# Second half of batch 0 by full-height matmuls, its values regrouped by transfers, expert 1's first chunk earlier

## The chip, the cores and the metric

The kernel runs on one core of a Trainium2 chip. The metric is the device time of one execution in microseconds (us); lower is better. A core has a matrix engine (PE, TensorE), three engines for element work (DVE, ACT, POOL), and SP, which issues transfers. POOL issues transfers too, and these can change the number type on the way. Each engine takes its instructions in a fixed order; between engines, semaphores tell when a result is there or a buffer is free. PE writes into PSUM, and ACT or DVE copy from there into SBUF, the working memory.

## The reference

The input is `q`, `k`, `v` of shape (4 batches, 8 heads, 768 tokens, 64), a small matrix `sort_net` of 8x8 for each batch and head, and a mixture of four experts.

```python
P = sort_net                                  # (B, H, 8, 8)
for _ in range(5):                            # rows and columns normalized in turn
    P = exp(P - max(P, -1)); P = P / (sum(P, -1) + 1e-9); P = P / (sum(P, -2) + 1e-9)
k_sorted[b,h,i] = sum_j P[b,h,i,j] * k_block[b,h,j]      # blocks of 96 tokens
v_sorted[b,h,i] = sum_j P[b,h,i,j] * v_block[b,h,j]
attn = softmax(q_block k_sorted^T / 8)        # 96x96 inside each of the 8 blocks
x = attn v_sorted                             # (3072 tokens, 512): heads side by side
p = domain_probs / sum(domain_probs)          # (3072, 4)
out = sum_e p[:, e] * (relu(x @ w1[e]) @ w2[e])          # 512 -> 1024 -> 512
```

## The kernel before

All matrix work is in 16 bits with float sums. Batch 0 has code of its own, since the experts can't begin before its attention is there; batches 1 to 3 run their attention in slots between the matmuls of the experts (`PLANS`).

**Mixing as a matmul.** A head's keys lie in SBUF as 128 rows (8 blocks j times 16) of 6x64 values: token p*6+r is row p, part r. The mixing of blocks is then a product with a matrix that holds P[i,j] where the row inside the block agrees. `PI0[hf]` is this matrix for half `hf` of the output blocks (four of eight), 64 columns for a head, built from `maskk` and `Rs`.

**Batch 0 by halves.** Half 0 is the first four output blocks (tokens 0 to 383), half 1 the other four. The heads are in two quads (`qd`), each of two pairs (`sg`) of two heads (`hh`). For a quad and a half there are these steps (names as in the code):

- `h_q`: 24 transposes of 64x64 bring the queries into `qT0`.
- `h_k` and `h_v`: 24 matmuls each (`mix_half`, L495) with outputs of 64 partitions by 64 columns, then one copy (`mixed`, L506) into `kT` or `vT0`. The values come out with channels on partitions.
- `h_w`: 8 transposes (L522) turn the values to tokens on partitions, and a copy (L527) puts them into `vs0s`, beside a column of ones that gives the softmax sums.
- `h_s(qd, qq)`: scores of two blocks, 8 matmuls (L550) and one exponential on ACT (L556). `qq` is 0, 1 in half 0 and 2, 3 in half 1.
- `h_a(qd, qq)`: the product with the values, 8 matmuls (L567), then on DVE a reciprocal (L580) and a multiplication (L581) into `xsl`.
- `h_x(qq)`: 4 matmuls for each quad (L598) bring the result into `xT`, the input of the experts; the copy (L602) is on ACT or DVE.

PSUM results of these steps rotate through `psa`, a pool of two buffers; expert work has `psm`, another two. `ps_a10` is a buffer of `psa` that is used under several names (`ps_s11` too), the last time by `h_x(1, vec, [1], ps_s11)`.

**Experts for batch 0.** Expert 0 is done plainly: `group0` (L679) is its first layer for one half, `second_layer0` (L714) its second, one token tile of 128 after the other, each result scaled by `p_sb` on DVE (L723). Experts 1 to 3 go by chunks of 256 tokens: `chunk_first` (L790) is their first layer, two groups of 16 matmuls, each followed by a DVE step (L796) that applies relu and the weight row `pbs`. The second layers of these experts use sums of blocks (`h_sums`, `weight_sums`) and `product`.

**The order around the change.** After `h_a(1, 1)` come the two `h_k(qd, 1)`, with the groups of expert 0 between; then `h_v(0, 1)`, `h_q(0, 1)` and `second_layer0(0, next_stages)`. This calls `next_stages` after 4 and after 8 matmuls of each of its three tiles, and `chunk_first(0, 0, [1, 2], ...)` calls it after each of its four groups. Each call takes one entry of the list `later` (L1439): the rest of half 1's queries and values, its scores, its products, and at last `h_x(2)` and `h_x(3)`. `h_x(3)` stands before the last group of expert 2. Then `first_layer0(2, 2)` (L679) reads `xT` of half 1.

**Transfers.** POOL's queue has the loads of the weights (`load_w1`, `load_w2`) in the order of need, with tables between them (`builds`, the `memset` of `vo`, `maskv`). SP's queue has the way of the weights p: `spread_weights` is advanced by `next(p_steps)`; its last step multiplies, stores p to `p_dram`, loads `p_0` (expert 0's, as 6 rows of 128), the broadcast rows of all four experts (`load_p`) and stores the rest. `own_weights` turns `p_0` by a transpose on PE (L249). `load_p_one` follows for the second chunk.

**Borrowed room.** `Tt` are four tiles for the sums of expert weights, which are made later; until then they hold `q0` (in `Tt[3]`) and `p_in`, `p_out`, `p_0` (in `Tt[2]`).

## Time and profile before

| what | value |
|---|---|
| runs | 359.24, 359.61, 359.78 us; median 359.61 |
| span of the profiled execution | 357.8 us, 1.8 under the median of the runs |
| PE busy | 351.6 us (98%), clock 1.00 |
| DVE, ACT, POOL busy | 276.2, 170.6, 133.6 us |
| DMA share in the first 140 us | 8 to 9 tenths or more of 16 engines for nearly all of it |

The span runs from the first to the last instruction; what lies around it is not in the profile, and no time for the profiled execution itself is given beside the span. In the lines of the profile a row of the timeline has the start in us, the duration in us, engine, line, operation, output<-input, size, and the count of instructions that were merged into it. In brackets stands how long the engine was idle before it and what it waited for. Matmuls overlap, so the time that a group costs is the distance from its start to the next start. A row of windows has the stretch, then its length, then for each engine the busy time and the number of instructions, the TensorE clock that was granted, the DMA share and GB/s. A row of transfers has the queue that issued them, their count, the KB of each and the median us from issue to landing.

### The profile page before, as it was taken

The numbers are of one execution on the slowest core, as the hardware profiler recorded it, in microseconds if no ns is written. First come the engines' busy times: TensorE is split into PE (matmuls) and PEld (weight loads), VectorE is DVE, ScalarE is ACT, GpSimd is POOL, SyncE is SP. The second block draws the span as 40 slices with busy tenths as digits, with TensorE's granted clock in tenths as the row PEclk, the third lists the DMA queues.
The fourth block names the chain that finished last, engine by engine and source line by source line (L and its number), as shares of the span: only waits on it lengthen the run. The fifth ranks groups of instructions, "written<-read, shape, count | busy, mean of one in ns | idle before, by whom it ended". The sixth has DMA issues, their size and how long they took to land.

```text
span 357.8 us, 9498 instructions
## 1 busy us (share of the span) xinstructions
PE 351.6 (98%) x3949; PEld 306.3 (86%) x3949; DVE 276.2 (77%) x552; ACT 170.6 (48%) x303; POOL 133.6 (37%) x149
## 2 busy tenths in 40 slices
PE   8899999999999999999999999999999999999996
PEld 8686867888888888888899988888888888888886
DVE  5754797869889587868978988896678886588963
ACT  2554240442434535367947258830288611688201
POOL 8864010375122222000535318840058800188400
PEclk9999999999999999999999999999999999999999
DMA  8999999999999999935996420005200015100011
GB/s 114 207 205 228 216 210 198 209 163 165 201 154 160 188 152 170 194 74 73 168 201 90 102 78 0 2 2 108 102 29 2 3 39 138 61 0 2 2 73 46
DMA packets 72022, 40.51 MB, mean 113 GB/s; under 512 B 40614, under 2 KB 66732, under 8 KB 71980
## 3 DMA queue, kind: packets, MB, share of 16 engines
q0 software_dynamic: 36576, 19.93, 41.9%
q1 hardware_dynamic: 35260, 19.92, 28.5%
q8 instruction: 31, 0.51, 0.6%
q14 instruction: 11, 0.09, 0.1%
q10 hardware_dynamic: 144, 0.07, 0.1%
HBM read 42.13 MB, written 6.34 MB: 135 GB/s over the span
## 4 chain that ended last, share of the span: by engine, by line
PE 95%; DVE 2%; ACT 1%; DMA 0%; issue 0%; DVEq 0%
PE ps_h L790 18%; PE ps_Q L1264 18%; PE ps_p L774 12%; PE ps_X L1121 10%; PE ps_Z L1121 7%; PE ps_Q L1121 7%; PE ps_Z L1264 6%; PE ps_h L679 3%; PE ps_o L714 3%; PE ps_p L830 3%; PE ps_a L453 2%; PE ps_s L418 2%; PE ps_k L399 1%; PE ps_v L365 1%; PE ps_a L567 1%; PE ps_mk L495 1%
## 5 line engine op out<-in xcount | busy, mean ns | idle before, releaser
L790 PE MATMUL ps_h<-xT,w 128*128 128x256 f16 x576 | 67.5, 273 | 0.0
L790 PEld LDWEIGHTS <-w 128*128 128x128 f16 x576 | 55.2, 98 | 7.2
L796 DVE SCALAR_TENSOR_TENSOR Hb<-ps_h,pb 128x1024 f16<-128x1024 f32 x34 | 41.5, 1223 | 17.2 <-PE ps_h L790 15.8
L1121 PEld LDWEIGHTS <-w 128*128 128x128 f16 x480 | 43.6, 98 | 4.8
L1134 POOL TENSOR_TENSOR arena<-tmp,pb 128x512 f16<-128x512 f32 x12 | 15.2, 1275 | 65.7 <-PE ps_Z L1121 49.8
L1264 PEld LDWEIGHTS <-Hb 128*128 128x128 f16 x320 | 31.1, 98 | 3.5
L1133 ACT ACTIVATE tmp<-tmp 128x512 f32<-128x512 f32 x46 | 29.0, 632 | 3.9 <-DVE tmp L1171 3.9
L1264 PEld LDWEIGHTS <-Sb 128*128 128x128 f16 x304 | 28.3, 98 | 3.0
L1121 PEld LDWEIGHTS <-arena 128*128 128x128 f16 x312 | 27.7, 98 | 2.9
L425 ACT ACTIVATE ET<-ps_s 96x768 f16<-96x768 f32 x24 | 18.0, 802 | 25.1 <-PE ps_s L418 24.8
L121 POOL DMA_DIRECT2D arena<-in_q_dram x24 | 19.9, 838 | 25.5 <-DMA q_ring<-arena 25.2
L408 ACT CAST kT<-ps_k 64x384 f16<-64x384 f32 x48 | 22.7, 473 | 13.3 <-PE ps_k L399 12.3
L1121 PE MATMUL ps_X<-ET,arena 128*128 128x256 f16 x168 | 25.2, 272 | 0.0
L1264 PE MATMUL ps_Q<-w,Hb 128*128 128x256 f16 x192 | 24.6, 273 | 0.0
L774 PEld LDWEIGHTS <-Hb 128*128 128x128 f16 x232 | 21.8, 98 | 3.0
L1127 DVE SCALAR_TENSOR_TENSOR Hb<-ps_X,pb 128x512 f16<-128x512 f32 x27 | 18.7, 691 | 7.0 <-PE ps_X L1121 7.0
L1141 ACT COPY ps_X<-ps_Z 128x512 f32<-128x512 f32 x27 | 15.4, 571 | 17.8 <-PE ps_Z L1121 17.8
L1121 PE MATMUL ps_Z<-xT,w 128*128 128x256 f16 (+1 forms) x176 | 22.5, 258 | 0.0
L760 DVE TENSOR_TENSOR Sb<-Hb 128x512 f16<-128x512 f16 x33 | 20.6, 647 | 0.0
L1148 ACT COPY tmp<-ps_X 128x512 f32<-128x512 f32 x26 | 15.2, 585 | 9.2 <-PE ps_X L1121 6.6
L1127 DVE SCALAR_TENSOR_TENSOR Hb<-ps_Z,pb 128x512 f16<-128x512 f32 x27 | 18.4, 682 | 1.3 <-PE ps_Z L1121 1.3
L1171 DVE TENSOR_TENSOR tmp<-ps_Q,tmp 128x512 f32<-128x512 f32 x26 | 17.8, 683 | 0.8 <-PE ps_Q L1121 0.8
(266 smaller groups left out, 741.6 us busy)
## 6 DMA issues: line engine op xcount, KB each, us to landing
w<-in_moe_w_dram POOLq DMA_DIRECT2D x6, 1024.0 KB, 27.9
pb<-p_dram SPq DMA_DIRECT2D x9, 512.0 KB, 7.0
arena<-in_k_dram POOLq DMA_DIRECT2D x8, 384.0 KB, 9.3
arena<-in_v_dram POOLq DMA_DIRECT2D x8, 384.0 KB, 7.5
vs<-arena SPq DMA_DIRECT2D x36, 66.0 KB, 4.9
arena<-in_q_dram POOLq DMA_DIRECT2D x24, 96.0 KB, 7.5
out_dram<-ob SPq DMA_DIRECT2D x9, 256.0 KB, 2.0
w<-in_moe_w_dram POOLq DMA_DIRECT2D x4, 512.0 KB, 12.5
```

The lines of the kernel that those rows point to most:

```text
L121: nc.gpsimd.dma_start(t[:, h // 2, :, h % 2, :], q[b, h].rearrange("(t p) d -> p t d", p=P))
L408: nc.scalar.copy(kT[ds(D * hh, D), r], pk[ds(D * r, D), hh].rearrange("p a (i c) -> p a i c", c=CP),)
L425: nc.scalar.activation(ETs[2 * (pr % 2) + hh][:, 0:S].rearrange("c (a x) -> c a x", a=2), pss[hh][0:BLK, :, 0:HS], AF.Exp, bias=0.0, scale ...
L760: tt(sm[0], blk(0, 1), blk(1, 1), ALU.add)
L774: nc.tensor.matmul(ps, lhs(e, f), Ts[e][rhs][:, f, :], start=(first and e == es[0] and f == 0), stop=(done and e == es[-1] and f == KH - 1 ...
L790: nc.tensor.matmul(ps[:, f, :], w1sb[e][:, kc, ds((4 * g + f) * P, P)], xT[:, kc, ds(2 * c * P, 2 * P)], start=(kc == 0), stop=(kc == NKC ...
L796: nc.vector.scalar_tensor_tensor(out=Hb[:, homes.get(e, e), ds(4 * g, 4), :], in0=ps[:], scalar=0.0, op0=ALU.max, in1=weights(e).broadcast ...
L1121: nc.tensor.matmul(dst[:, ds(f * cols, cols)], a[lhs][:, k, ds((f0 + f) * P, P)], t[rhs][:, k, :], start=(first and f == 0 and k == 0), st ...
L1127: nc.vector.scalar_tensor_tensor(out=home(i, j), in0=src.rearrange("p (f x) -> p f x", f=m), scalar=0.0, op0=ALU.max, in1=weight(j).broadc ...
L1133: nc.scalar.activation(src, src, AF.Relu, bias=0.0, scale=1.0)
L1171: tt(t12, Q, u2, ALU.add)
L1264: nc.tensor.matmul(ps, lhs(e, f), Ts[e][rhs][:, f, part], start=(first and e == 0 and f == 0), stop=(e == E - 1 and f == KH - 1), skip_gro ...
```

## The change

The queries, keys and values of half 1 are done in another way, and the steps around them are put in another order.

- `half_v` replaces `h_v` and `h_w` for half 1: two matmuls for a pair of heads, each with 64 columns of weights (`PIv1`, 4 output blocks times 16) and 384 columns of values. Tokens come out on partitions at once, but as 16 times 4 (c, i). A copy on ACT puts them into `vo1s[qd]`; after the quad's second pair six transfers on SP (one for each r) regroup them into `vs1s[qd]`, 96 partitions. `vs1s` and one of `vo1s` lie in `Tt[0]` and `Tt[1]`. `PIv1` lies in `Tt[2]` and is built on POOL, from `maskv`.
- `half_k` replaces `h_k` for half 1: 12 matmuls with 128 by 128 weights (two parts r at a time) and 64 columns, and four copies.
- `pair_q` and `half_q` replace `h_q` for half 1: two copies on ACT into `q1`, 12 full transposes for both quads, and two copies on DVE.
- `h_a` for half 1 reads `vs1s`.
- POOL's `maskv`, the build of `PIv1` and the two `memset` of `vo1s` stand ahead of `load_w1(1)`; before, `maskv` and one `memset` stood behind `load_w1(2)`.
- The weight rows of chunk 0 come one expert at a time; `spread_weights` has two steps more, taken between the parts of `half_v`, so that SP has the row of expert 1, six value transfers, the row of expert 2, six more, the row of expert 3 and the rest of the store. The row of expert 0 is not loaded for batch 0.
- `own_weights` is a plain float matmul of 128 rows (`p_0` has zeros below its 6 rows) in place of a transpose.
- `second_layer0` takes the tiles to do: two tiles, then expert 1's first chunk, the third tile, then expert 2's. The list `later` is new, and its last entries are `h_a(1, 2)` with `h_a(1, 3)`, and `h_x(2)` with `h_x(3)`.

```diff
@@ -206,18 +206,27 @@
 
     p_dram = dramp.tile([E, N], F32, name="p_dram")
     p_sb = const.tile([P, R, 1], F32, name="p_sb")
-    p_0 = p_part(2 * E * NT + NT, P)[0:R]
-    ident6 = p_part(2 * E * NT + NT + P, R)[0:R]
+    p_0 = p_part(2 * E * NT + NT, P)
+    ident6 = p_part(2 * E * NT + NT + P, R)
+    nc.gpsimd.memset(p_0, 0.0)
     S_P = S // NT
 
     pbs = {}
 
+    def load_p_rows(pb, b, c, es):
+        nc.sync.dma_start(
+            pb[:, es],
+            p_dram[es, ds(b * S + 2 * c * P, 2 * P)].rearrange("(o e) x -> o e x", o=1).broadcast_to(
+                [P, es.stop - es.start, 2 * P]
+            ),
+        )
+
+    def new_p(b, c):
+        return moe.tile([P, E, 2 * P], F32, name=f"pb_{b}_{c}", tag="pb", bufs=1)
+
     def load_p(b, c):
-        pb = moe.tile([P, E, 2 * P], F32, name=f"pb_{b}_{c}", tag="pb", bufs=1)
-        nc.sync.dma_start(
-            pb[:],
-            p_dram[:, ds(b * S + 2 * c * P, 2 * P)].rearrange("(o e) x -> o e x", o=1).broadcast_to([P, E, 2 * P]),
-        )
+        pb = new_p(b, c)
+        load_p_rows(pb, b, c, slice(0 if b else 1, E))
         return pb
 
     def load_p_one(b, c, e):
@@ -239,14 +248,18 @@
         )
         p_rows = p_dram.rearrange("e (p t) -> p e t", t=NT)
         nc.sync.dma_start(p_rows[0:S_P], p_out[0:S_P])
-        nc.sync.dma_start(p_0, p_dram[0, 0:S].rearrange("(t p) -> t p", p=P))
-        pbs[(0, 0)] = load_p(0, 0)
+        nc.sync.dma_start(p_0[0:R], p_dram[0, 0:S].rearrange("(t p) -> t p", p=P))
+        pbs[(0, 0)] = new_p(0, 0)
+        for e in range(1, E):
+            load_p_rows(pbs[(0, 0)], 0, 0, slice(e, e + 1))
+            if e < E - 1:
+                yield
         nc.sync.dma_start(p_rows[S_P:P], p_out[S_P:P])
         yield
 
     def own_weights(ps):
 
-        nc.tensor.transpose(ps, p_0, ident6)
+        nc.tensor.matmul(ps, p_0, ident6, start=True, stop=True)
         nc.vector.tensor_copy(p_sb.rearrange("p t o -> p (t o)"), ps)
 
 
@@ -279,7 +292,7 @@
     sn16 = const.tile([GH, NB, NB, CP], F16, name="sn16")
     warm(84)
     p_steps = spread_weights()
-    nc.gpsimd.tensor_copy(ident6, ident[0:R, 0:R])
+    nc.gpsimd.tensor_copy(ident6, ident[:, 0:R])
     for it in range(5):
         nc.scalar.activation(sn[:], sn[:], AF.Exp, bias=0.0, scale=1.0)
         if it == 4:
@@ -514,6 +527,88 @@
     def h_v(qd, hf, copy, pool=psa):
         mixed("v", qd, mix_half("v", qd, hf, pool), 0, HB, copy)
 
+    def flat_T(e, at, n):
+        return Tt[e].rearrange("p a f x -> p (a f x)")[:, ds(at, n)]
+
+    NVO, NVS, NQ1 = R * 4 * VW, HB * 4 * VW, 2 * R * P
+    vo1s = [vo, flat_T(0, 0, NVO).rearrange("p (r h w) -> p r h w", r=R, h=4)]
+    vs1s = [
+        flat_T(e, at, NVS)[0:BLK].rearrange("c (i s h w) -> c i s h w", i=HB, s=2, h=2)
+        for e, at in ((0, NVO), (1, NQ1))
+    ]
+    PIv1 = flat_T(2, 3 * KH * DH - H * CP * HB, H * CP * HB).rearrange("p (h c i) -> p h c i", h=H, i=HB)
+
+    def build_PIv1(eng):
+        eng.tensor_tensor(
+            PIv1,
+            maskv.rearrange("p (o c i) -> p o c i", o=1, i=NB)[:, :, :, 0:HB].broadcast_to([P, H, CP, HB]),
+            Rs[:, 0:H, HB:NB].rearrange("p g (o i) -> p g o i", o=1).broadcast_to([P, H, CP, HB]),
+            ALU.mult,
+        )
+
+    def half_v(qd, sg, copy):
+
+        ps = psa([P, 2, 512], F32, f"ps_v0_{qd}_{sg}")[0:CP * HB]
+        for hh in range(2):
+            h = 2 * sg + hh
+            nc.tensor.matmul(
+                ps[:, hh, 0:R * D],
+                PIv1[:, 4 * qd + h].rearrange("p c i -> p (c i)"),
+                head(0, "v", 4 * qd + h).rearrange("p r d -> p (r d)"),
+                start=True, stop=True,
+            )
+        vo1 = vo1s[qd][0:CP * HB]
+        copy(
+            vo1[:, :, ds(2 * sg, 2), 0:D],
+            ps[:, :, 0:R * D].rearrange("p h (r d) -> p r h d", r=R),
+        )
+        if sg:
+            for r in range(R):
+                nc.sync.dma_start(
+                    vs1s[qd][ds(r * CP, CP)].rearrange("c i s h w -> c (i s h w)"),
+                    vo1[:, r].rearrange("p h w -> p (h w)"),
+                )
+
+    def half_k(qd, copy):
+
+        ps = psa([P, 2, 512], F32, f"ps_k0_{qd}")
+        pk = ps[:, :, 0:R * 64].rearrange("p h (x i c) -> p h x i c", x=R, c=CP)
+        for hh in range(2):
+            for sg in range(2):
+                h = 4 * qd + 2 * sg + hh
+                for a in range(R // 2):
+                    nc.tensor.matmul(
+                        ps[:, hh, ds((sg * (R // 2) + a) * 64, 64)],
+                        head(0, "k", h)[:, ds(2 * a, 2), :].rearrange("p r d -> p (r d)"),
+                        PI0[1][:, h, :, :].rearrange("p i c -> p (i c)"),
+                        start=True, stop=True,
+                    )
+        kT = kTs[qd][:, 0:S].rearrange("p (i x r c) -> p r x i c", i=HB, r=2, c=CP)
+        for hh in range(2):
+            for r in range(2):
+                copy(kT[ds(D * hh, D), r], pk[ds(D * r, D), hh])
+
+    q1 = flat_T(1, 0, NQ1).rearrange("p (s r x) -> p s r x", s=2, r=R)
+
+    def pair_q(sg):
+
+        nc.scalar.copy(
+            q1[:, sg].rearrange("p r (h d) -> p r h d", h=2),
+            q0[:, 1, ds(2 * sg, 2)].rearrange("p h r d -> p r h d"),
+        )
+
+    def half_q(copy):
+
+        ps = psa([P, 2, 1024], F16, "ps_q1")
+        for sg in range(2):
+            for r in range(R):
+                nc.tensor.transpose(ps[:, sg, ds(r * P, P)], q1[:, sg, r], ident[:])
+        for qd in range(2):
+            copy(
+                qT0[qd][:, :, 1],
+                ps[:, :, 0:R * P].rearrange("p s (r q x) -> p s r q x", r=R, q=2)[:, :, :, qd],
+            )
+
     def h_w(qd, copy, i0=0, n=HB, at=None):
 
         ps = psa([P, n, 2 * P], F16, f"ps_w_{state['n']}") if at is None else at
@@ -567,7 +662,7 @@
                 nc.tensor.matmul(
                     ps[:, hh, ds(n * VW, D + 1)],
                     ET[:, ds((4 * hh + n) * BLK, P)],
-                    vs0s[qd][:, 2 * (qq % 2) + n % 2, n // 2, hh, 0:D + 1],
+                    (vs0s, vs1s)[qq // 2][qd][:, 2 * (qq % 2) + n % 2, n // 2, hh, 0:D + 1],
                     start=True, stop=True,
                 )
 
@@ -705,8 +800,8 @@
             group0(qq, nq, g)
             slot()
 
-    def second_layer0(hf, slot):
-        for t in range(R // 2):
+    def second_layer0(hf, slot, ts=range(R // 2)):
+        for t in ts:
             col = (R // 2) * hf + t
             po = psm([P, 2, 512], F32, f"ps_o_{col}")
             ps = po[:, 0, 0:Dm]
@@ -1373,6 +1468,13 @@
     load_half_queries(1)
     load_w2(0, 2)
     build_PI0(nc.gpsimd, 1, 0, H, Rs[:, 0:H, HB:NB])
+    nc.gpsimd.tensor_copy(
+        maskv.rearrange("p (c i) -> p c i", i=NB),
+        eye16.rearrange("p (c o) -> p c o", o=1).broadcast_to([P, CP, NB]),
+    )
+    build_PIv1(nc.gpsimd)
+    for t in vo1s:
+        nc.gpsimd.memset(t[:, :, :, ds(D, 2)], 1.0)
     h_w(0, vec, 0, 2, tails[("v", 0, 0)])
     mixed("v", 0, mv0, 2, 2, vec)
     mk1 = mix_half("k", 1, 0, psm)
@@ -1407,23 +1509,22 @@
     h_x(1, act, [0], ps_s01)
     evacuate00()
     group0(0, 1, 1, [2, 3])
+    load_w1(1)
+    load_w1(2)
     h_a(1, 1, ps_s11)
-    h_k(0, 1, act)
+    half_v(0, 0, act)
     group0(1, 1, 0, [0, 1])
+    half_v(0, 1, act)
+    next(p_steps)
     h_x(1, vec, [1], ps_s11)
     group0(1, 1, 1, [0, 1])
-    h_k(1, 1, vec)
+    half_v(1, 0, act)
     group0(1, 1, 0, [2, 3])
+    half_v(1, 1, act)
+    next(p_steps)
     group0(1, 1, 1, [2, 3])
-
-
-    load_w1(1)
-    load_w1(2)
-    nc.gpsimd.memset(vo[:, :, :, ds(D, 2)], 1.0)
-    nc.gpsimd.tensor_copy(
-        maskv.rearrange("p (c i) -> p c i", i=NB),
-        eye16.rearrange("p (c o) -> p c o", o=1).broadcast_to([P, CP, NB]),
-    )
+    for sg in range(2):
+        pair_q(sg)
 
     def builds(b):
         for n in range(2 * b, 2 * b + 2):
@@ -1437,15 +1538,16 @@
     builds(1)
 
     later = [
-        [(h_q, 1, 1, vec)],
-        [(h_v, 1, 1, act)],
-        [(h_s, 0, 2), (h_w, 1, vec)],
-        [(h_w, 0, vec), (h_s, 1, 2)],
+        [(half_k, 1, act)],
+        [(half_q, vec)],
+        [(h_s, 0, 2)],
+        [(h_s, 1, 2)],
+        [(h_s, 0, 3)],
+        [(h_s, 1, 3)],
         [(h_a, 0, 2)],
-        [(h_s, 0, 3), (h_a, 1, 2)],
-        [(h_s, 1, 3), (h_a, 0, 3)],
-        [(h_x, 2, act), (h_a, 1, 3)],
-        [(h_x, 3, act)],
+        [(h_a, 0, 3)],
+        [(h_a, 1, 2), (h_a, 1, 3)],
+        [(h_x, 2, act), (h_x, 3, act)],
     ]
 
     def next_stages():
@@ -1453,14 +1555,15 @@
             for f, *args in later.pop(0):
                 f(*args)
 
-    h_v(0, 1, act)
-    h_q(0, 1, vec)
-    second_layer0(0, next_stages)
+    half_k(0, vec)
+    second_layer0(0, next_stages, range(2))
+    chunk_first(0, 0, [1], 1, next_stages)
+    second_layer0(0, next_stages, range(2, 3))
     load_queries(1, range(2))
     for qd in range(2):
         for nm in ("v", "k"):
             load_natural(1, nm, qd)
-    chunk_first(0, 0, [1, 2], 1, next_stages)
+    chunk_first(0, 0, [2], 1, next_stages)
     pb_1 = load_p_one(0, 1, 1)
     h_sums(1, 4)
     for w in range(1, 5):
```

## The prediction

> **What bounds the kernel now.** I read the page's busy times and its chain first, then the stage that the change touches by windows, then that stage's timeline on each engine, then the DMA view.
>
> ```profile
> PE 351.6 (98%) x3949; PEld 306.3 (86%) x3949; DVE 276.2 (77%) x552; ACT 170.6 (48%) x303; POOL 133.6 (37%) x149
> ...
> PE 95%; DVE 2%; ACT 1%; DMA 0%; issue 0%; DVEq 0%
> ```
> TensorE is busy for the whole span and is 95% of the chain that ends last. A microsecond taken from its queue is worth a microsecond, but so is a gap put into it.
>
> ```profile
> 23.20:46.20 23.00, 23.00 (x376) 17.48 (x374) 14.45 (x24) 9.93 (x13) 8.51 (x10) 1.00 1.20 219
> ```
> The stage that changes runs from the end of head group 1's second attention product (23.52 us) to the layer of expert 0's second half (46.19). In this window TensorE (first busy figure) is busy for 23.00 of 23.00 us, at clock 1.00; DVE has 14.45, ACT 9.93. No TensorE wait over 0.2 us stands in it, nor any after 46.2. The stage has no slack to win, only work.
>
> ```profile
> 23.52 0.57 PE L495 MATMUL ps_mk<-Sb,arena 128*64 128x64 f16 x24
> 24.02 0.83 PE L679 MATMUL ps_h<-xT,w 128*128 128x192 f16 x8
> ...
> 29.50 0.56 PE L271 MATMUL ps_q<-ident,T 64*64 64x64 f16 x24
> 30.00 1.04 PE L714 MATMUL ps_o<-w,Hb 128*128 128x512 f16 x4
> ...
> 32.87 0.65 PE L522 MATMUL ps_w<-ident,Sb 128*96 128x128 f16 x8
> 33.35 1.03 PE L714 MATMUL ps_o<-w,Hb 128*128 128x512 f16 x4
> ...
> 44.10 0.51 PE L598 MATMUL ps_x<-perm,xsl 96*128 96x96 f16 x8
> 44.44 1.91 PE L790 MATMUL ps_h<-xT,w 128*128 128x256 f16 x16
> 46.19 5.54 PE L679 MATMUL ps_h<-xT,w 128*128 128x384 f16 x32
> ...
> 65.05 0.49 PE L365 MATMUL ps_v<-arena 128*128 128x384 f16 x2
> 65.37 1.47 PE L830 MATMUL ps_p<-w,Hb 128*128 128x256 f16 x12
> ```
> Start to start gives what a group costs: 24 half-width products 0.50 us, 24 query transposes 0.50, 8 value transposes 0.48. The last h_x ends before 16 expert matmuls (44.44), which cover the copy of its result; only then does the next layer read it.
>
> **TensorE's work.** Removed for the second half: h_k twice, h_v twice, h_q twice at 0.50 each, h_w at 0.48 and 0.54: 4.02 us. Added:
> - half_v, 4 calls of two 384-column matmuls: row 65.05, 0.33 each (0.32 to 0.33 start to start): 1.32.
> - half_k, 2 calls of 12 matmuls of 64 columns. No row has 128 rows by 64 columns; bounds are 21 ns (L495, 0.50/24) and 55 ns (128 columns, L399, 6 in 0.33). The h_a products with 65 columns are nearest, 8 in 0.25, 31 ns: 0.74 in all (0.50 to 1.32).
> - half_q, 12 full transposes: 60 ns by L522: 0.72 (0.66 to 0.80).
> - own_weights now loads 128 float rows instead of 6 for 6 columns: 0.15 before, not shown after; 0.15 to 0.54 (four of its weight loads, 134 ns each, in a row), taken 0.30 between them, so +0.15.
>
> Net 1.32+0.74+0.72+0.15-4.02 = **-1.09 us**, -0.2 to -1.5 at the ends. The Trainium skill (TensorE: Matmul & The Clock Gate, Back-to-back issue gap) states about 81 ns for each 128-column matmul with its weights in a sustained stream. By it half_q would be 0.97, the net -0.84; the 55 and 60 ns rows here are shorter, and I go by them.
>
> **The waits it adds.** I walked the changed order with durations of this trace, an end and the next start 0.04 us apart.
>
> ```profile
> 23.09 1.52 ACT L692 ACTIVATE Hb<-ps_h 128x768 f16<-128x768 f32 x2
> ...
> 44.64 0.80 ACT L602 CAST xT<-ps_x 128x768 f16<-128x768 f32 x1 [1.54 <-PE ps_x L598]
> ...
> 65.57 0.80 ACT L371 CAST arena<-ps_v 128x768 f16<-128x768 f32 x1
> ...
> 68.85 1.96 ACT L408 CAST kT<-ps_k 64x384 f16<-64x384 f32 x4 [0.85 <-PE ps_k L399]
> ```
> *First, half_v.* All four results are copied by ACT (0.80 each by L371). The other buffer of the pool of two is held by ps_a10 until h_x(1, [1]), so by the built order half_v(0,1) takes half_v(0,0)'s buffer and half_v(1,0) takes half_v(0,1)'s: each waits for the copy before it. ACT has the two L692 to do until 24.61, so copy (0,0) is 24.51 to 25.31. TensorE starts half_v(0,0) at 23.52, expert 0's group at 23.94 (its buffer is free at 23.90), needs 0.67 for it, is at half_v(0,1) at 24.61 and goes on at 25.35: **0.74**. Behind it stand h_x(1, [1]), expert 0's groups and all that follows. 0.33 half_v, 0.17 h_x and 0.75 group later it is 26.60; half_v(1,0) waits for the copy that ends at 26.67: **0.11**. ACT then has copy, L692, copy, L692 until 30.18.
>
> The Trainium skill (Perfetto Trace Analysis, Optimizing Tensor Performance, Matmuls) says that independent groups should rotate through PSUM banks so that an evacuation overlaps the next group's matmuls; half_v does not here. With a free buffer at that rotation the 0.85 would be nothing; by the 0.80 rows it is 0.85.
>
> *Second, keys and queries.* ACT does two pair_q copies (0.78 each, to 31.6; not shown from SBUF, bounds 0.56 for the DVE copy of the same size and 0.95 for 768 elements at L1133's 632 ns per 512), then half_k(1) as four 64x384 copies: 1.96, to 33.46. h_s(0,2) takes that buffer. TensorE, from 26.71: twice half_v and a group (0.33+0.71), twice half_k and half a second layer (0.37+0.87), own_weights 0.30, half_q 0.72, half a second layer 0.97: there at 33.26, goes at 33.50: **0.23** (0 to 0.6 with the bounds). half_k(0)'s four copies on DVE (0.56 each) end at 31.3, before half_q. With h_s, half a layer, h_s (0.28+0.97+0.28) expert 1's first group starts at 35.03; two groups and two h_s (1.84+0.28 each), two half layers and two h_a (0.87+0.25, 0.87+0.26) bring expert 2's first group to 41.52.
>
> *Third, the tail.* Here it decides. The order now puts h_a(1,2) and h_a(1,3) between expert 2's groups and both h_x after the last of them, directly before the layer that reads their result.
>
> ```profile
> 41.97 1.22 DVE L796 SCALAR_TENSOR_TENSOR Hb<-ps_h,pb 128x1024 f16<-128x1024 f32 x1 [0.32 <-PE ps_h L790]
> 43.11 0.19 DVE L580 RECIPROCAL rz<-ps_a 96x8 f32<-96x8 f32 x1
> 43.34 0.69 DVE L581 TENSOR_TENSOR xsl<-ps_a,rz 96x512 f16<-96x512 f32 x1
> ```
> DVE, from the end of expert 2's first group (41.52+1.91 = 43.43): the L796 step 1.14 start to start, one sum 0.34, then two normalizations one after the other (0.23+0.63, then 0.23+0.69): xsl for (1,2) at 45.86, for (1,3) at 46.72. TensorE ends the second group at 45.52 (1.75+0.50 for two h_a+1.75), waits for the first normalization (**0.38**), does h_x(2) in 0.34, waits for the second (**0.52**), ends h_x(3) at 47.27; ACT copies 0.80 (L602) to 48.10; the layer starts at 48.14, **1.04** after TensorE had nothing left. Before, the 16 matmuls at 44.44 covered that copy.
>
> Sum: waits 0.74+0.11+0.23+0.38+0.52+1.04 = 3.02; work -1.09; small steps of the walk +0.02: **+1.95**, the layer at 48.14 against 46.19. After it the order is that of before and TensorE had no wait there that could give this back.
>
> **What stays covered.** POOL builds PIv1 before w1 of expert 1 is issued: about 1.05 (a 128x512 build) plus 0.5 of copy and memsets, so the issue moves from 16.39 to about 18. Before, that load landed 17.1 us after its issue, behind the loads ahead of it (the DMA share is 9 tenths throughout), so about 33.5 still; a full 1.6 later would be 35.1, 0.1 past the need at 35.0. POOL stood idle 2.28 at 19.2 to 21.5 waiting for a load, so the later issues do not move. w1 of expert 2 landed at about 39.7 and is needed at 41.5.
>
> On SP, p_0 still leaves at 26.2, then row 1 of the weights, six value transfers, row 2, six more, row 3, the rest of the store, and load_p_one:
>
> ```profile
> pb<-p_dram SPq DMA_DIRECT2D x9, 512.0 KB, 7.0
> vs<-arena SPq DMA_DIRECT2D x36, 66.0 KB, 4.9
> ...
> T<-p_dram SPq DMA_DIRECT2D x1, 128.0 KB, 14.4
> ```
> Before, SP issued 512, 36 and 128 KB from 26.55 on and the last landed at 27.6+14.4 = 42.0. Now the second set of values (six transfers of 34 KB, 203 KB) is behind 128+203+128 KB: 662 KB, so also about 42, against h_a(1,2) at 43.3; the first set (331 KB) about 34 to 37, against 40.1. Bounds for the last transfer: issued at about 36 (it waits for earlier ones), 4.9 makes 41, 14.4 makes 50.4. Nothing, or up to 7 us; I take nothing, since the bytes ahead of it are the same. load_p_one then lands some 10 us later than 42 and is needed at 60.7. Row 1 is the first of SP's broadcasts: 512 KB landed after 11.7, at 38.2, a quarter of it should at about 30 to 33, and expert 1's first result needs it at 36.9. Batch 1's queries landed at about 61 before and may come 2 later by the added 405 KB; their readers are 2 later too.
>
> **Rivals.**
> - *The values land late* (same side): above; each us after 44.3 adds one. At 50.4 it is 6.1 more, 367.7; halfway 364.6. Against it: the bytes on SP.
> - *The tail is hidden* (not slower): if DVE and ACT finish 1.9 us sooner after expert 2's first group than my chain of 4.71 (43.43 to 48.14), TensorE never waits for h_x, and +1.95-1.94 is nothing: 359.6. It decides at a chain under 2.8 us. Against it: the durations alone are 1.14+0.34+0.23+0.63+0.23+0.69+0.51+0.80 = 4.57.
> - *Only the work counts*: no wait binds, -1.09: 358.5. It needs ACT's copies and the tail to be free at once.
>
> **How the numbers follow.** The span of 357.8 lies 1.8 under the median of the runs, 359.61; I keep that difference, so 357.8+1.95+1.8 = **361.6**. My forecast's three groups of waits get 0.74, late values 0.12, a hidden tail 0.08, work alone 0.06. Spread of the first: work +-0.4, pair_q and half_k +-0.5, tail +-0.4: 360.6 to 362.8. The range reaches down to a half-hidden tail and up into late values: 360.2 to 363.4. The measurement cannot tell under 0.2%, 0.72 us. Slower by more: 0.74+0.12 = 0.86; within: 0.08; faster: 0.06.
>
> **What would show it.** In the changed profile: TensorE gaps of 0.7 near 25 (released by ACT's ps_v copy), 0.2 near 33.5, and three near 46 to 48 released by DVE xsl and ACT xT; the 384-column layer of expert 0 at 48.1. A gap at h_a released by the value transfers would be the first rival; that layer at 45 would be the last. I would be wrong most if ACT's queue runs ahead of my walk, or if half_v does not share the buffer.

## The result and the profile after

| kernel | median of the runs | lowest to highest | ratio to the kernel before |
|---|---|---|---|
| before, beside it | 359.75 us | 359.24 to 361.90 | |
| changed | 363.11 us | 362.06 to 363.54 | 1.0091 (95% interval 1.0070 to 1.0113) |

The changed kernel is 0.9% slower, about 3.3 us, where the prediction had 361.6 us and a range of 360.2 to 363.4. The profiled execution took 363.54 us, its span is 361.7, so again 1.8 us lie around the span. Lines from `half_v` on stand 95 further down in the changed file: `group0` and the first layer are L774, `second_layer0` is L809, `chunk_first` L885, `h_a` L662, `h_x` L693.

First the busy times and the chain of the changed kernel's page:

```profile
PE 351.1 (97%) x3834; PEld 304.5 (84%) x3834; DVE 276.1 (76%) x553; ACT 174.5 (48%) x310; POOL 134.9 (37%) x152
...
PE 90%; ACT 4%; DVE 3%; issue 1%; DMA 0%; ACTq 0%; DVEq 0%
```

PE is busy for 351.1 us, hardly less than before (351.6), while the span is 3.9 longer, and ACT and DVE now have 7% of the chain, against 3%: the time is in waits, not in matmuls. The stage itself, measured from the start of `h_a(1,1)` to the start of expert 0's 384-column layer, by windows. Before:

```profile
23.18:46.19 23.01, 23.01 (x375) 17.49 (x374) 14.45 (x24) 9.95 (x14) 8.50 (x10) 1.00 1.20 219
```

After:

```profile
22.86:47.97 25.11, 22.80 (x261) 16.01 (x259) 15.80 (x28) 13.92 (x21) 8.83 (x10) 1.00 1.21 217
```

The stretch grew from 23.01 to 25.11 us, **+2.10**, with the clock at 1.00 in both; PE goes from no idle time to 2.31 us of it. The timeline of PE in the changed kernel shows where:

```profile
23.20 0.51 PE L554 MATMUL ps_v<-arena,T 128*64 128x384 f16 x2
23.64 0.83 PE L774 MATMUL ps_h<-xT,w 128*128 128x192 f16 x8
25.01 0.48 PE L554 MATMUL ps_v<-arena,T 128*64 128x384 f16 x2 [0.53 <-ACT arena L561]
...
31.12 0.28 PE L262 MATMUL ps_o<-T 128*128 128x6 f32 x2
31.70 0.83 PE L605 MATMUL ps_q<-ident,T 128*128 128x128 f16 x12 [0.30 <-DVE kT L589]
...
41.34 1.91 PE L885 MATMUL ps_h<-xT,w 128*128 128x256 f16 x16
43.56 0.64 PE L662 MATMUL ps_a<-T,ET 96*128 96x65 f16 x16 [0.32 <-PE ps_h L885]
44.04 1.91 PE L885 MATMUL ps_h<-xT,w 128*128 128x256 f16 x16
45.79 0.51 PE L693 MATMUL ps_x<-perm,xsl 96*128 96x96 f16 x8
46.57 0.51 PE L693 MATMUL ps_x<-perm,xsl 96*128 96x96 f16 x8 [0.28 <-DVE xsl L676]
47.97 0.81 PE L774 MATMUL ps_h<-xT,w 128*128 128x384 f16 x4 [0.89 <-ACT xT L697]
```

Two forecast waits are there with their releasers: `half_v(0,1)` behind ACT's copy at 25.01, and the layer behind ACT's copy of `xT` at 47.97, with DVE's normalization ahead of `h_x(3)` at 46.57. The chain that ends in the layer, on DVE and ACT:

```profile
43.29 1.23 DVE L891 SCALAR_TENSOR_TENSOR Hb<-ps_h,pb 128x1024 f16<-128x1024 f32 x1 [0.41 <-PE ps_h L885]
44.76 0.20 DVE L675 RECIPROCAL rz<-ps_a 96x8 f32<-96x8 f32 x1
44.99 0.69 DVE L676 TENSOR_TENSOR xsl<-ps_a,rz 96x512 f16<-96x512 f32 x1
45.83 0.69 DVE L676 TENSOR_TENSOR xsl<-ps_a,rz 96x512 f16<-96x512 f32 x1
46.33 1.59 ACT L697 CAST xT<-ps_x 128x768 f16<-128x768 f32 x2 [6.24 <-PE ps_x L693]
```

From the end of expert 2's first group (43.25) DVE does its own step, then two normalizations one after the other (to 45.68 and 46.52), `h_x(3)` waits for the second, and the last of ACT's copies, 0.80 each, ends at 47.92. Past the stage there is something that the prediction does not have:

```profile
169.16 4.23 SPq L379 DMA_DIRECT2D vs<-arena  x6
179.13 0.65 PE L453 MATMUL ps_a<-vs,ET 96*128 96x65 f16 x16
...
171.02 5.38 SPq L392 DMA_DIRECT2D vs<-arena  x6
182.53 0.64 PE L466 MATMUL ps_a<-vs,ET 96*128 96x65 f16 x16 [1.47 <-ACT arena L1092]
```

The first two lines are the kernel before, the last two the changed one. At 182.5 us, in batch 1, PE stands idle for 1.47 us before an attention product (before: at 179.13, no wait). The product reads values that six transfers of SP bring; SP took 5.38 us to issue them, 4.23 before. The releaser that the row names has no part in these values. The sixth transfer, issued at 174.2, landed 8.2 us later by the trace, at 182.4, just ahead of the product: it is what the product waited for.

So the two profiles differ by 3.9 us: -0.32 ahead of the stage, +2.10 in it, -0.18 in the layer behind it (5.38 to 5.20 us), +0.17 at a group near 173, +1.63 at the wait near 182, and +0.51 after the last store's issue, where the span ends 3.34 us later instead of 2.83.

### The profile page after: what moved, and what is told of

Its sections match the earlier page's. It is cut to its first block, busy times and chain, and to the rows that moved or that the text cites. A ratio compares the mean times of both kernels' runs of the same rounds, so it can differ in the third digit from the quotient of the medians.

```text
span 361.7 us, 9314 instructions
## 1 busy us (share of the span) xinstructions
PE 351.1 (97%) x3834; PEld 304.5 (84%) x3834; DVE 276.1 (76%) x553; ACT 174.5 (48%) x310; POOL 134.9 (37%) x152
## 4 chain that ended last, share of the span: by engine, by line
PE 90%; ACT 4%; DVE 3%; issue 1%; DMA 0%; ACTq 0%; DVEq 0%
PE ps_h L885 18%; PE ps_Q L1359 17%; PE ps_p L869 10%; PE ps_X L1216 10%; PE ps_Z L1216 7%; PE ps_Q L1216 7%; PE ps_Z L1359 6%; PE ps_h L774 3%; PE ps_p L925 3%; PE ps_o L809 2%; PE ps_a L466 2%; PE ps_s L431 1%; PE ps_k L412 1%; ACT arena L1092 1%; PE ps_v L378 1%
## 5 line engine op out<-in xcount | busy, mean ns | idle before, releaser
L885 PE MATMUL ps_h<-xT,w 128*128 128x256 f16 x576 | 67.5, 273 | 0.0
L885 PEld LDWEIGHTS <-w 128*128 128x128 f16 x576 | 55.1, 98 | 7.3
L421 ACT CAST kT<-ps_k 64x384 f16<-64x384 f32 x48 | 22.7, 473 | 13.6 <-PE ps_k L412 11.8
```

The lines of the kernel that those rows point to most:

```text
L421: nc.scalar.copy(kT[ds(D * hh, D), r], pk[ds(D * r, D), hh].rearrange("p a (i c) -> p a i c", c=CP),)
L885: nc.tensor.matmul(ps[:, f, :], w1sb[e][:, kc, ds((4 * g + f) * P, P)], xT[:, kc, ds(2 * c * P, 2 * P)], start=(kc == 0), stop=(kc == NKC ...
```

## The experiments

Where a run is compared by stage, the measure is the distance from the start of `h_a(1,1)` to the start of the layer, 23.01 us before and 25.11 after. What lies ahead of it changes from run to run in both kernels (`h_a(1,1)` started between 22.7 and 24.8 us), and the distance does not.

**1. Again.** No edit.

> The changed kernel once more, nothing edited. Theory: the stage of the change always costs the same, with the 384-column layer of expert 0 starting 1.8 us later than before (near 47.97), because its waits follow from fixed durations; the further 1.8 us that the first profile showed at 182.5 us (a wait of 1.47 at st_a(3,2)) hang on when batch 1's last value transfers land, which is not the same in every execution: five timed spans of that kernel ran from 360.3 to 361.7. So a second profile should have the stage's part again, and may lack the wait near 182; times from 361.8 to 363.6. Rival A: the wait near 182 belongs to the change as firmly as the stage does; then it stands here again, 1.3 to 1.6 us, and the shift against the kernel before is +3.4 at the end. Rival B: the landing of the regrouped values (0.32 us of idle at 43.56 in the first profile) is the random part; then that idle changes by more than 0.3 while the rest stays.

363.15 us, 1.0081 (1.0055 to 1.0107). The stage took 25.11 again, the same waits within 0.04, and the idle ahead of `h_a(1,2)` fell from 0.32 to 0.14 without the layer coming sooner. So that idle varies, as rival B has it, but it moves nothing. The wait near 182 was there with 1.17, SP's six issues took 5.15; rival A stays open.

**2. Without the use of the regrouped values.**

```diff
-                    (vs0s, vs1s)[qq // 2][qd][:, 2 * (qq % 2) + n % 2, n // 2, hh, 0:D + 1],
+                    vs0s[qd][:, 2 * (qq % 2) + n % 2, n // 2, hh, 0:D + 1],
```

> The changed kernel, but the attention products of batch 0's second half read the first half's values, so what is left out is the use of the regrouped values; the transfers are still made, nobody waits for them. Theory: their landing costs 0.32 us (the idle at 43.56), and a part of it is won back by the waits that follow: the layer of expert 0 starts at 47.6 to 47.8 instead of 47.97; the time 0.1 to 0.4 below the changed kernel. Rival: values that land late are what makes the kernel slower (the whole +1.8 of the stage): then the layer starts near 46.2 and the time falls by 1.5 or more. If instead nothing changes at all, the two normalizations by the vector engine set the end of the stage whenever the values land.

364.01 us, 1.0097 (1.0070 to 1.0124).

```profile
46.15 0.51 PE L693 MATMUL ps_x<-perm,xsl 96*128 96x96 f16 x8 [0.25 <-DVE xsl L676]
...
195.46 0.62 PE L1216 MATMUL ps_X<-kT,arena 128*128 128x128 f16 x8 [0.59 <-DMA arena<-arena]
197.82 0.62 PE L1216 MATMUL ps_Q<-xT,w 128*128 128x128 f16 x8 [0.86 <-DMA w<-arena]
```

The stage took 25.10. The third possibility holds: `h_a(1,2)` has no wait now, but the first `h_x` has one of 0.25 in its place, and from expert 2's first group to the layer it is 6.62 us against 6.63. The chain over DVE sets the end, so the landing of the values cost the changed kernel nothing in this stage. My 0.1 to 0.4 was a miss: I had counted an idle time as a price. This profile has no wait near 182, but two others, of 0.59 and 0.86 us, behind transfers at 195 and 198.

**3. The same, with both `h_x` ahead of expert 2's last group.**

```diff
-        [(h_a, 0, 2)],
-        [(h_a, 0, 3)],
+        [(h_a, 0, 2), (h_a, 0, 3)],
         [(h_a, 1, 2), (h_a, 1, 3)],
         [(h_x, 2, act), (h_x, 3, act)],
```

> As the kernel without the use of the regrouped values, and with the list of later steps put in another order: both h_a of the first quad pair after expert 1's last group, both h_a of the second after expert 2's first group less one, and both h_x ahead of expert 2's last expert group, which then lies over the copy of their result, as it did in the kernel before. Theory: the tail (0.28 at h_x(3) and 0.89 at the layer) is the greatest of the waits, so the layer starts 1.1 to 1.4 us sooner than in the kernel without the use of the values, near 46.4, and the whole is within 0.4 us of the kernel before, or 1.3 to 2.2 over it if the wait near 182 shows. Rival: the normalizations and copies are late anyway; then the waits only move from the layer to h_x, 0.8 to 1.2 us of idle ahead of the last expert group, and the layer still starts near 47.6.

361.37 us, 1.0049 (1.0027 to 1.0071). PE's timeline of this run:

```profile
43.38 0.42 PE L662 MATMUL ps_a<-Sb,ET 96*128 96x65 f16 x8 [0.42 <-DVE xsl L676]
43.63 1.91 PE L885 MATMUL ps_h<-xT,w 128*128 128x256 f16 x16
45.38 0.85 PE L693 MATMUL ps_x<-perm,xsl 96*128 96x96 f16 x16
46.06 1.91 PE L885 MATMUL ps_h<-xT,w 128*128 128x256 f16 x16
47.81 0.98 PE L774 MATMUL ps_h<-xT,w 128*128 128x384 f16 x5
```

The layer follows the group without a wait; the stage, which began late at 23.99 here, took 23.82. The tail is worth 1.29 us, and 0.42 of wait came back at `h_a`. The wait near 182 was 0.47.

**4. Own rows for the second pair of `half_v`.** Both pairs of a quad in one buffer, rows 0 to 63 and 64 to 127.

```diff
-        ps = psa([P, 2, 512], F32, f"ps_v0_{qd}_{sg}")[0:CP * HB]
+        if not sg:
+            both_v[qd] = psa([P, 2, 512], F32, f"ps_v0_{qd}")
+        ps = both_v[qd][ds(CP * HB * sg, CP * HB)]
```

> The changed kernel with one edit: both head pairs of a half_v quad go into one PSUM buffer, rows 0 to 63 and rows 64 to 127, so that the second pair needs no copy before it; everything is computed. Theory: the idle of 0.53 at 25.01 ahead of half_v(0,1), and nearly all of the 0.7 from the end of the group before it, goes; the steps after it come 0.5 to 0.7 sooner until half_q, where TensorE waits for the vector engine's four copies of keys, which hang on nothing of this: there the gap grows from 0.30 towards 0.6. The layer of expert 0 at 47.4 to 47.9. Rival: half_v(1,0) then waits as long for the copy that now frees its buffer (the second one of quad 0), so that the idle moves from half_v(0,1) to half_v(1,0) and the sum of the two stays at 0.5 to 0.7.

363.47 us, 1.0111 (1.0080 to 1.0142), and both expectations missed:

```profile
25.31 0.48 PE L558 MATMUL ps_v<-arena,T 128*64 128x384 f16 x2 [0.54 <-ACT arena L565]
```

The wait stayed, and `half_v(1,1)` came 0.18 later after the step before it than in the changed kernel (0.94 against 0.76); the stage took 25.27. The built program makes the second pair wait for the copy out of the same buffer whatever its rows, so the edit did not take the wait away and says nothing on its price.

**5. `half_v(0,1)` later.**

```diff
     group0(1, 1, 0, [0, 1])
-    half_v(0, 1, act)
-    next(p_steps)
     h_x(1, vec, [1], ps_s11)
     group0(1, 1, 1, [0, 1])
+    half_v(0, 1, act)
+    next(p_steps)
     half_v(1, 0, act)
```

> The changed kernel with one move: half_v(0,1) comes after h_x(1, [1]) and expert 0's next group, directly ahead of half_v(1,0), so that the copy of half_v(0,0) (24.17 to 24.96 on ScalarE) is over before TensorE needs its buffer; nothing is left out. The edit before it, rows 64 to 127 of the same buffer, left the idle at 0.54, since the built program waits for the copy of the buffer and not of its rows. Theory: the wait at half_v(0,1) (0.7 from the end of the group) and the small one at half_v(1,0) go, half_k(0) starts 0.6 to 0.95 sooner after half_v(0,0) than 28.69-23.20 = 5.49; at the end of the stage 0.4 to 0.9 is left, because expert 2's first group may then wait for its weights (landed near 40.9, the group would start near 40.4 instead of 41.34): half_v(0,0) to the layer 23.9 to 24.4 instead of 24.77. Rival: the copies of the four half_v are the bound, not the one wait: then the idle turns up at half_v(1,1) or half_k, half_k(0) starts at the same distance from half_v(0,0) within 0.2, and so does the layer.

361.94 us, 1.0075 (1.0062 to 1.0089).

```profile
25.26 0.84 PE L554 MATMUL ps_v<-arena,T 128*64 128x384 f16 x4
...
27.91 0.51 PE L580 MATMUL ps_k<-Sb,arena 128*128 128x64 f16 x12
...
34.60 1.92 PE L885 MATMUL ps_h<-xT,w 128*128 128x256 f16 x16 [0.28 <-DMA w<-in_moe_w_dram]
...
47.72 1.46 PE L774 MATMUL ps_h<-xT,w 128*128 128x384 f16 x8 [0.89 <-ACT xT L697]
```

The wait is gone and `half_k(0)` starts 4.75 us after `half_v(0,0)` instead of 5.49, 0.74 sooner, which is what the prediction had for the wait. The Trainium skill asks for just such a rotation of buffers (Perfetto Trace Analysis, Optimizing Tensor Performance, Matmuls), and this run agrees with its 0.74. But only 0.22 reach the layer (24.89 from `h_a(1,1)`, or 24.56 from `half_v(0,0)`, short of the 23.9 to 24.4 expected): 0.18 go at `h_s(0,2)`, and 0.35 at expert 1's first group, which now comes so soon that it waits for its weights; they landed at about 34.5. All twelve transfers are made and used here, and this profile has no wait near 182.

**6. Keys and queries alone.** The kernel before with `half_k`, `pair_q` and `half_q` for `h_k` and `h_q`.

```diff
-    h_k(0, 1, act)
+    half_k(0, act)
...
-    h_k(1, 1, vec)
+    pair_q(0)
+    half_k(1, vec)
...
-        [(h_q, 1, 1, vec)],
         [(h_v, 1, 1, act)],
+        [(half_q, vec)],
...
-    h_q(0, 1, vec)
```

> The kernel before with the keys' and queries' part of the change alone (half_k for h_k, half_q with its two copies for h_q); values, loads, the list of later steps and the tail as before; nothing is left out. Theory: the work of these parts is shorter by 1.00-0.70 = 0.30 us (keys) and 1.00-0.67 = 0.33 us (queries), and the h_x steps stay under expert 2's last group, so the stage from the end of h_a(1,1) to the layer takes 22.0 to 22.4 instead of 22.67, the layer starts 0.3 to 0.65 sooner, and the time is 0.1 to 0.6 below the kernel before. Rival: full-height work in this place brings its copies with it (half_k(0) by four copies of ScalarE, two pair copies of 0.78 each), so that a new wait of the size of the one at half_v appears and the stage is no shorter than 22.67.

359.65 us, 1.0016 (0.9997 to 1.0035), beside 359.57 for the kernel before: no difference that can be told.

```profile
22.98 0.51 PE L530 MATMUL ps_k<-Sb,arena 128*128 128x64 f16 x12
23.52 0.82 PE L724 MATMUL ps_h<-xT,w 128*128 128x192 f16 x8
...
27.71 1.02 PE L759 MATMUL ps_o<-w,Hb 128*128 128x512 f16 x4 [0.16 <-ACT Hb L737]
```

The stage took 22.92 against 23.01, and 22.67 from the end of `h_a(1,1)`, the rival's number to the hundredth. It did not come by one wait, as the rival had it: of the 0.63 us that are saved in matmuls, small waits took back most: 0.19 at 23.52 (`half_k` costs 0.35, the next start is 0.54 later), 0.14 before the second `half_k` (0.08 in the old order), 0.23 at 27.71 where expert 0's second layer waits for an ACT step behind the key copies, 0.12 at `h_w`.

**7 and 8. The step behind the late wait, one slot sooner**, in the changed kernel and in the kernel before.

```diff
-            (1, 7, st_k, 3, 3), (1, 8, st_v, 3, 3), (1, 9, st_a, 3, 0),
+            (1, 7, st_v, 3, 3), (1, 7, st_k, 3, 3), (1, 9, st_a, 3, 0),
```

> The changed kernel with one step of batch 1 moved, far behind the change: st_v(3,3), whose six transfers SP issues ahead of st_a(3,2), goes one slot sooner, ahead of st_k(3,3); nothing is left out. In the four profiles of the changed order the wait at st_a(3,2) was 1.47, 1.17, 0.47 and 0 where SP took 5.38, 5.15, 4.78 and 4.53 us to issue these six. Theory: the wait is theirs and falls on some executions of the changed kernel; sooner transfers take it away in all, so the times gather at the lower end of the changed kernel's (361.8 to 362.3), the median 0.8 to 1.4 us lower than the changed kernel's 363.1, and the shift of TensorE's work against the kernel before stays at +1.5 to +2.1 past 182 us. Rival: another transfer near 180 to 200 is the late one (in one profile the idle stood at 195.5 and 197.8 instead, at steps that wait for transposes and queries by DMA); then the median stays within 0.4 of 363.1 and the idle only moves.

> The kernel before with that same step of batch 1 moved and nothing else. Theory: the kernel before has the same weak spot with some 0.3 to 0.9 us more room; 4 of its 16 last times were over 360.5 where the others were 359.2 to 360.1. With the transfers sooner these high times should go or halve, and the median stay at 359.4 to 359.8, or be up to 0.3 higher where the moved step itself costs something. Rival: the move costs TensorE a wait of its own (st_v ahead of st_k): then the median rises by 0.4 or more, and a gain in the changed kernel is partly hidden by it.

363.96 us, 1.0108 (1.0087 to 1.0129), and 360.65 us, 1.0032 (1.0017 to 1.0047). In the changed kernel's profile the stage took 25.11 and the wait near 182 is gone, as the theory had it. The median did not fall, but it can't decide what the move is worth. Four of the six executions, the profiled one among them, had a granted clock of 0.995 over the span; the two at 1.00 took 362.08 and 362.58. In the profile the stage starts at 24.83, 1.97 later than in the changed kernel's, after a granted clock of 0.50 between 18 and 20 us, far ahead of the moved step. And in the kernel before the move costs about 1 us by itself, so a gain would be partly hidden. That the wait is for these transfers is seen in the traces all the same: in the first profile and in run 1's the sixth lands 8.2 and 7.9 us after its issue at 174.2 and 174.0, each time 0.1 ahead of the product.

**9. The other order with the regrouped values in use.** The edit of the third run alone.

> The changed kernel with the list of later steps in the other order (both h_x ahead of expert 2's last expert group), everything computed, so h_a(1,2) now needs the regrouped values of the second quad pair. With half 0's values in their place this order took 23.82 us from h_a(1,1) to the layer, against 25.11 for the changed kernel, and h_a(1,2) began 18.56 us after h_a(1,1). Theory: with the regrouped values, which the first profile of the changed kernel shows landed at 43.2 to 43.5 (20.4 to 20.6 after h_a(1,1)), h_a(1,2) begins that late, an idle of 1.6 to 2.2 us released by the transfers stands ahead of it, and the layer comes 25.4 to 26.1 after h_a(1,1): no better than the changed kernel, or up to 1 us worse. So the late h_x of the change is the price of the transfers, and the two cannot be cured apart. Rival: the values had landed well before and the 0.32 of idle at 43.56 was something else; then the interval is 23.7 to 24.1 and the time 1.0 to 1.4 below the changed kernel's.

363.51 us, 1.0114 (1.0066 to 1.0161).

```profile
43.99 0.91 PE L662 MATMUL ps_a<-T,ET 96*128 96x65 f16 x16 [2.61 <-DMA T<-T]
44.70 3.32 PE L885 MATMUL ps_h<-xT,w 128*128 128x256 f16 x16
```

Right in kind: the transfers release `h_a(1,2)`, 21.3 us after `h_a(1,1)`, and the stage is longer, 27.56, than the 25.4 to 26.1 that I gave. The profile is of the longest of the four executions, 366.66 us. 2.61 of idle were more than my 2.2, and the group behind it took 3.16 us from start to start where it takes 1.75. The granted clock (the third figure from the end) tells why:

```profile
41.30:44.00 2.70, 0.09 (x2) 0.04 (x2) 1.39 (x3) 0.00 (x0) 0.00 (x0) 1.00 1.21 222
44.00:45.00 1.00, 1.00 (x18) 0.94 (x19) 0.47 (x2) 0.00 (x0) 0.00 (x0) 0.59 1.36 217
45.00:46.00 1.00, 1.00 (x7) 0.69 (x6) 0.97 (x3) 0.00 (x0) 0.00 (x0) 0.50 1.45 214
```

**10. Both cures, without the use of the regrouped values** (the edits of runs 2, 3 and 5).

> Both cures of the stage in one kernel: half_v(0,1) behind expert 0's next group, and the later steps in the other order; as in the run with that order alone the second half's attention products of batch 0 read the first half's values, so the use of the regrouped values is left out. Theory: the two waits are separate, so the savings add, 25.11-1.29-0.74 = 23.08 us from h_a(1,1) to the layer, to which the waits for expert 1's weights (0.28 of idle in the run with the first cure alone) and for half_k's copies add 0.2 to 0.6: 23.1 to 23.7, against 23.01 before the change. So even freed of its two waits and of its transfers' landing the new work is no shorter than the old in this place. Rival: with both waits gone the shorter work shows, the sum of the prediction's work term less what half_v and own_weights took more (-1.09+0.42 = -0.67), and the interval is 22.2 to 22.7.

361.05 us, 1.0043 (1.0019 to 1.0067). The stage took 23.25, as expected: with the tail out of the way the first cure is worth 0.57 (23.82 to 23.25). Without its two large waits, and without waiting for its transfers, but with 0.30 still at `half_q` and 0.42 at `h_a`, the new work is still not shorter than the old. The run's median is nevertheless 1.4 above the kernel before, with 0.70 of wait near 182 in its profile.

**11. Two transfers more**, so that the last stores take the same turn in the row of eight semaphores as before.

```diff
-        nc.sync.dma_start(p_rows[S_P:P], p_out[S_P:P])
+        S_Q, S_R = S_P + (P - S_P) // 3, S_P + 2 * (P - S_P) // 3
+        for r0, r1 in ((S_P, S_Q), (S_Q, S_R), (S_R, P)):
+            nc.sync.dma_start(p_rows[r0:r1], p_out[r0:r1])
```

> The changed kernel with the last store of the row weights to DRAM, near 27 us, cut into three by rows, so that SP and ScalarE issue two transfers more in all; nothing is left out. What is tested lies at the far end: in every profile with the value transfers the span ends 3.3 us after the last store's issue, in those without (the kernel before, and the one with keys and queries alone) 2.8. Transfers take their semaphores in turn from eight, and at the end SP waits for the eight one after the other; the change issues 14 transfers more, which puts the last stores on other places in that row, two more bring them back to the places that they had. Theory: the distance from the last store's issue to the end of the span goes back to 2.7 to 2.9, the time is 0.5 below what the stage and the late waits make of it, the lowest times come near 361.3 instead of 361.8. Rival: the 0.5 has nothing to do with the order of these waits (a longer landing of the stores): it stays at 3.2 to 3.4.

362.25 us, 1.0079 (1.0049 to 1.0109). The span ended 3.20 us after the last store's issue, against 3.34 and 2.83. The order of the waits explains 0.14 of the 0.51 at most; the theory falls for the rest. Nor do the stores land later, as its rival had it: the last one lands 1.6 us after its issue in the changed kernel and in the one before. What takes longer is SP's row of waits behind it, whose last one stands 2.4 us after that issue in the changed kernel, 2.3 here, 1.9 before.

**12. Without the twelve transfers.** The second run's edit, and the `dma_start` in `half_v` taken out.

> The changed kernel whose second half of batch 0 reads the first half's values (as in the run without the use of the regrouped values), and now the twelve transfers that regroup them are not made either: left out are the transfers and their use; every matrix product, copy and load stays. Theory: the stage is bound by TensorE's work, the wait at half_v(0,1) and the tail, none of which hangs on the transfers, so h_a(1,1) to the layer stays at 25.1 (25.11 and 25.10 in three runs, transfers made). Open is what makes the times of the changed kernel spread: its median lies 1.3 above its lowest time, that of the kernel before 0.5. If the transfers and the traffic behind them are the cause, then without them no wait over 0.3 stands at st_a(3,2) and the times gather within 0.6 of the lowest, median 361.8 to 362.3. Rival: the late waits come with anything that shifts batch 1 against its loads, or by chance; then the spread stays, median 362.8 to 364.0. For the end of the span: with two transfers more than before the change (row weights in parts) the distance from the last store's issue to the end is 2.8 if the twelve transfers were its cause, 3.2 to 3.4 if not.

361.63 us, 1.0061 (1.0039 to 1.0083); all six runs between 361.34 and 362.29.

```profile
47.95 2.27 PE L768 MATMUL ps_h<-xT,w 128*128 128x384 f16 x13 [0.89 <-ACT xT L691]
180.89 0.64 PE L466 MATMUL ps_a<-vs,ET 96*128 96x65 f16 x16
```

The stage is again 25.11. But the 0.17 near 173 is gone, the wait near 182 is 0.18 at most, and the span ends 2.67 us after the last store's issue. Against the second run, which differs in these transfers alone, the median is 2.4 us lower; against the two medians of the changed kernel it is 1.5 lower. About 0.7 of this is the end of the span (3.35 us after the last store's issue in run 2, 2.67 here), and every profile agrees: 3.2 to 3.4 in the ten with the transfers, 2.7 to 2.9 in the four without. The rest is late waits, and whether these are the transfers' is not shown. The two runs were on different chips, where the kernel before took 359.67 and 359.41. The waits change from execution to execution of one kernel, and among the profiles with the transfers those of runs 4 and 5 have none; run 5's median, 361.94, is within 0.3 of this one, with a stage 0.22 shorter. The sixth transfer near 175 landed 5.8 us after its issue here, 6.6 in run 2 and 5.3 in run 5, and SP took 4.83 us to issue the six, 4.23 before and 4.30 in run 2. So the transfers cost nothing where they are, some 0.7 us at the end, and perhaps up to 1.7 more some 140 us later.

## Why the prediction was right, and where not

The sign and the place were right: the kernel is slower, by waits that outweigh the shorter work. By the prediction's own terms, in us:

| term | predicted | measured in the changed kernel |
|---|---|---|
| TensorE's work | -1.09 | -0.78: `half_v` 1.74 instead of 1.32 (0.42 to 0.45 each), `half_k` 0.70, `half_q` 0.67, `own_weights` +0.13 |
| `half_v(0,1)` behind ACT's copy | 0.74 | 0.70 (24.31 to 25.01) |
| `half_v(1,0)` | 0.11 | 0.10, and 0.09 more at `half_v(1,1)` |
| `h_s(0,2)` behind `half_k(1)`'s copies | 0.23 | 0 |
| `half_q` behind `half_k(0)`'s copies | 0 | 0.30 |
| tail: `h_x(2)`, `h_x(3)`, layer | 0.38+0.52+1.04 | 0.47 at `h_a(1,2)` instead of `h_x(2)`, 0.44, 1.06 |
| the stage | +1.95 | +2.10 |
| after the stage | 0 | -0.18+0.17+1.63+0.51 in the first profile |

The measured rows come to 2.38; of the 0.28 beyond 2.10, small gaps of some 0.08 each that the old order had at two groups (25.53 to 25.61, 27.46 to 27.54) are 0.16. Of the steps that both orders have, the second-layer halves came 0.20 shorter and the expert groups 0.13 longer.

- **The work.** The mis-sized term is `half_v`: I took 0.33 from L365, a 384-column pair with 128 columns of weights; with 64 columns of weights the pair takes 0.42 to 0.45. `half_q` is 12 transposes in 0.67, 56 ns each, under the 60 that I took.
- **The waits.** The shared buffer and the tail are shown by what their removal saved: 0.74 and 1.29 in runs 5 and 3. DVE's copies of `half_k(0)` end at 31.55; the walk had them at 31.3, before `half_q`, on a stage that began 0.32 later than this one did. A wait at `h_s(0,2)` then had nothing left.
- **The transfers.** "I take nothing" for the landing was right for the stage (run 2), though the second set had landed only at 43.2 (43.8 in run 9), later than my 42. Not only the bytes ahead of it timed it: in the first profile SP issued each of these six transfers only within 0.1 us after the landing of the one eight places before it on its queue, the last at 37.69 after a landing at 37.67. The rival of late values did not decide; run 9 shows that it does in run 3's order.
- **The other side.** "The tail is hidden" and "only the work counts" did not occur. Run 3 shows the first as a kernel of its own and still slower.
- **The step that failed**, beside the size of `half_v`, is "After it the order is that of before and TensorE had no wait there that could give this back". It looked for waits that could give something back, and not for slack that could be used up. About 1 to 1.5 us of the 3.3 are there: 0.5 at the end, which the added transfers bring (run 12), and the rest in late waits for a transfer of batch 1, whose cause stays open. The median, 363.1, lies 1.5 over my 361.6 for this reason; the stage without it, by run 12, makes 361.6. That the median is still in the range is partly luck: its upper end was there for late values in this stage, which cost nothing, and the sum for the stage came within 0.15 because its errors went both ways.

What stays open: why the sixth transfer of batch 1's values lands 5.3 us after its issue in one profile and 8.9 in another, and whether the twelve added transfers make this more frequent. Its issue took 1.07 us in the kernel before, 1.98 and 2.21 in the profiles with 1.17 and 1.47 of wait. High times occur without the transfers too: of the 16 executions of the kernel before beside runs 1 to 4, four took 360.5 to 361.5 where the others took 359.2 to 360.1. Open is also why SP's last row of waits takes longer with the transfers; run 11 takes away one explanation for most of it. I can't tell either whether the weight rows in parts have a share in run 12's remaining spread.

## What to carry to other kernels

Count a move by what it uncovers: the same normalizations and copy cost nothing under 16 matmuls and 1.3 us without them, and one wait's cure shows at the end only when the next one is also cured. Saved matmul time in a chain of short steps is easily lost again to the copies that the new shape needs. And look for the price of an added transfer beyond its own reader: here the reader lost nothing, and the end of the span came some 0.7 us later.

## What the runs showed of the hardware that was not expected

- An idle time of 2.61 us was followed by a granted clock of 0.59, 0.50, 0.50 and 0.70 in the next four microseconds (run 9), which cost 1.4 us more. In run 7 the clock fell to 0.50 between 18 and 20 us after gaps of at most 0.95 us in a stretch with little work (0.90 us between 14 and 16); run 3, with 1.12 there, kept 1.00. The Trainium skill (TensorE: Matmul & The Clock Gate, Why this matters for your kernels) sets the limit for gaps at about 3 us; by these runs shorter ones can be enough.
- A pair of 384-column matmuls takes 0.33 us with 128 columns of weights and 0.42 to 0.45 with 64 (0.77 for two such pairs in a row, run 5), so half the output partitions were not cheaper here but dearer.
- Twelve small transfers moved the end of the span by 0.5 to 0.7 us against the last store, which stands 320 us behind them, though that store landed 1.6 us after its issue with and without them.
